# Other ranks for 733 planned steps, and other engines for eleven copies, in a recurrent-attention and token-mixing kernel on one core

## The chip, the core and the metric

The kernel runs on one core of one Trainium2 chip. The metric is the device time of one execution in microseconds (us), lower is better. The core has five instruction queues that run side by side and wait for each other only through semaphores: PE (matmul, with its weight loads shown apart as PEld), DVE (vector), ACT (scalar and activation), POOL (GpSimd) and SP, which here issues the transfers between HBM and on-chip memory. Each queue is strictly in order: an instruction that waits holds everything behind it on its engine.

## What is computed

A decayed linear attention runs over 768 positions for 4 batches of 8 heads of width 48. Its output, with the heads side by side (width 384), goes through a token mixer.

```python
for t in range(S):                       # attention, per batch and head
    cur = einsum('bhd,bhe->bhde', u[None] * kt, vt)
    y[:, :, t] = einsum('bhd,bhde->bhe', rt, state + cur)
    state = wt[:, :, :, None] * state + einsum('bhd,bhe->bhde', kt, vt)
...
wq, wk = x @ w_q, x @ w_k                # mixer, x: [4, 768, 384]
W_tok = (1 / sqrt(64)) * einsum('bsd,btd->bst', wq, wk)
out = maximum(einsum('bst,btd->bsd', W_tok, x), 0) @ w_out
```

## The kernel before

**Tiling.** The work is cut into 12 units of 256 positions (two chunks of 128, called c0 and c1): unit n belongs to batch n // 3. Units 2, 5, 8 and 11 end a batch, and after them the mixer runs for the whole batch. The first and the last unit run chunk by chunk in several steps. In this text "10:KT" is step KT of unit 10, "11:x1" the second chunk of step x, and "5:os2" is step os for the third block of 256 output rows of the batch that unit 5 ends.

**The steps of a unit**, in the order of its data, with the function that issues each:
- Four loads from HBM, w, k, r and v, of 384 KB each. In seven of the twelve units (the string DIRECT) v comes as four transfers of 96 KB (L226), otherwise as one (L230).
- ln (ACT, L467) takes the logarithm of w; cw (PE) sums it along the chunk; en and ep (ACT, L498 and L504) are its exponentials.
- k16 and r16 (L475) cast k and r to bf16. kT and rT (PE) transpose them; ks (a copy, L371 on ACT or L375 on DVE) and qT (DVE, L529) follow.
- RT (DVE, L536) and KT (L547, DVE or POOL) are r and k with their decay. ptm (POOL, L553) is the decay of a chunk.
- v16, vp, vb, or vb alone where v came directly (POOL, L562), make the bf16 tile VB.
- dps (PE), dd (a small copy) and vd (POOL, L601) are the term with u.
- A (PE) and am (DVE, L619) are the masked product inside a chunk; kb (PE) and kd (L373 on ACT, L377 on DVE) the transposed keys; sn (PE) and sb (DVE, L666) the new state; y (PE) and x (DVE, L707) the output of the attention.
- xt (PE), xts (copy), qk (PE), qks (copy; in unit 11 split into qk1 and qk2 for each chunk) begin the mixer.
- At the end of a batch: T (PE) and Ts (ACT, L784), then for each of three blocks mx (PE), rl (L381 ACT, L383 DVE), fp (PE), os (copy) and st, the store of 384 KB (L838).
- "warm" steps are matmuls on zeros that nothing reads.

**What sets the order.** Every step is put on one of the five queues with a rank. The list RANK, written out by hand, gives each step its place: the steps of an engine are issued in the order of their ranks, and ranks are compared only within one engine. The dictionary ENG says, with one letter for each unit (A, D or P for ACT, DVE or POOL), where a step runs that can run on several engines (for rl and os the letter is that of the block). Plan.order() then walks the queues with its own estimates of durations. It can't change the order on an engine, but it hands out the eight PSUM banks by these estimates. The function add (inside unit) registers a step, copy issues it on the engine chosen.

**Buffers.** Loads rotate over four tiles for each input. The output tile os also has four: block m of the whole run (m = 0 to 11) uses tile m mod 4, so 5:os1 (m = 4) can be written only when the store of 2:os0 has left that tile, and 5:os2 when that of 2:os1 has. VB, KT, Vd, dd and their like have two tiles each.

Of the kernel before, what the change touches and what calls it, by code (L numbers as in the profile page):

```python
# [149 lines left out]
def kernel(  # L150
# [137 lines left out]
    for j in range(2):  # L288
# [9 lines left out]
               KT=-956, ptm=-433, v16=-873, vp=-305, vb=-304, dps=-1398, vd=-510, A=-1752,  # L298
               am=2180, kb=370, kd=2179, sn=-276, sb=-57, y=-127, x=-406, xt=-2208, xts=-634,
               qk=796, qks=-45, T=-761, mx=134, rl=-215, fp=-10, os=-8, st=95, stick=-14)  # L300
    ENG = dict(k16="DAPPAPPPPPPP", r16="DPPPPAPPPPPP", KT="DDPDPPPPPPPP", vb="AAAADAAAAAAA",
               kd="AAADAAAAADAA", xts="ADDADAADAAAD", qks="AAADAAAAAAAA", rl="AAAAAAAAAAAA",
               os="AAAAAAADDDDD", dd="AAAAAADDAAAD", ks="DDAAADADDAAD")
    RANK = [14, 0, 0, 0, 0, 15, 0, 0, 0, 1, 0, 0, 2, 0, 0, 5, 0, 0, 0, 0, 1, 1, 3, 1, 5, 2, 5, 10,
            2, 5, 4, 3, 2, 7, 6, 4, 1, 20, 9, 21, 11, 6, 7, 14, 8, 17, 9, 15, 10, 19, 12, 24, 13,
            23, 37, 17, 30, 15, 47, 23, 59, 33, 13, 28, 8, 89, 45, 55, 31, 4, 40, 32, 16, 38, 9,
            6, 11, 46, 75, 2, 3, 29, 69, 91, 43, 25, 7, 68, 3, 0, 0, 4, 0, 0, 6, 0, 0, 9, 0, 0, 4,
            6, 3, 12, 7, 8, 18, 22, 10, 14, 12, 11, 8, 9, 34, 16, 35, 18, 13, 41, 19, 33, 16, 27,
            15, 44, 20, 48, 57, 25, 49, 22, 56, 26, 61, 30, 8, 0, 0, 7, 0, 0, 10, 0, 0, 15, 0, 0,
            13, 5, 10, 36, 19, 17, 26, 39, 14, 21, 18, 14, 12, 16, 50, 24, 17, 54, 24, 51, 23, 52,  # L310
            25, 60, 27, 62, 63, 29, 67, 32, 73, 37, 80, 41, 90, 45, 102, 52, 42, 0, 0, 87, 44,
            104, 53, 49, 0, 0, 109, 56, 114, 59, 53, 0, 0, 12, 0, 0, 11, 0, 0, 17, 0, 0, 18, 0, 0,
            20, 11, 18, 53, 27, 26, 42, 66, 22, 33, 31, 28, 21, 19, 70, 34, 74, 36, 23, 72, 35,
            71, 34, 64, 30, 76, 36, 82, 81, 39, 83, 40, 92, 46, 97, 46, 13, 0, 0, 16, 0, 0, 20, 0,
            0, 22, 0, 0, 21, 29, 22, 58, 28, 31, 65, 79, 32, 38, 37, 20, 26, 25, 84, 42, 27, 88,
            42, 93, 44, 77, 38, 86, 41, 98, 94, 45, 99, 47, 107, 54, 113, 58, 19, 0, 0, 21, 0, 0,
            25, 0, 0, 28, 0, 0, 35, 24, 47, 78, 39, 40, 85, 100, 43, 48, 49, 30, 29, 34, 106, 54,
            35, 110, 56, 117, 58, 101, 51, 115, 57, 121, 122, 61, 128, 66, 133, 69, 139, 74, 149,
            79, 154, 82, 54, 0, 0, 151, 80, 162, 86, 52, 0, 0, 168, 89, 173, 92, 51, 0, 0, 23, 0,
            0, 24, 0, 0, 27, 0, 0, 30, 0, 0, 43, 28, 32, 96, 49, 50, 95, 103, 48, 51, 50, 33, 36,  # L320
            37, 116, 60, 108, 53, 40, 111, 55, 127, 64, 112, 57, 120, 60, 131, 125, 63, 132, 68,
            137, 71, 147, 78, 29, 0, 0, 26, 0, 0, 31, 0, 0, 36, 0, 0, 55, 31, 38, 118, 61, 63,
            105, 119, 52, 59, 65, 41, 43, 46, 124, 67, 47, 134, 69, 140, 72, 130, 68, 138, 70,
            144, 143, 73, 146, 75, 155, 80, 169, 90, 33, 0, 0, 32, 0, 0, 35, 0, 0, 38, 0, 0, 62,
            39, 42, 126, 65, 67, 123, 129, 62, 66, 71, 44, 45, 48, 136, 72, 50, 152, 78, 142, 74,
            135, 73, 148, 76, 156, 157, 81, 171, 91, 175, 93, 184, 101, 191, 104, 197, 107, 55, 0,
            0, 196, 106, 202, 106, 56, 0, 0, 201, 109, 210, 109, 57, 0, 0, 34, 0, 0, 39, 0, 0, 40,
            0, 0, 43, 0, 0, 64, 49, 51, 141, 76, 75, 145, 150, 77, 77, 79, 53, 57, 54, 160, 85,
            158, 83, 61, 163, 84, 159, 82, 161, 83, 166, 85, 177, 172, 90, 178, 92, 183, 100, 190,
            103, 37, 0, 0, 41, 0, 0, 46, 0, 0, 48, 0, 0, 70, 52, 56, 164, 87, 88, 153, 167, 81,  # L330
            86, 88, 59, 60, 62, 179, 95, 65, 174, 91, 181, 93, 176, 94, 182, 94, 188, 187, 97,
            189, 99, 195, 105, 198, 108, 44, 0, 0, 45, 0, 0, 47, 0, 0, 50, 0, 0, 84, 55, 58, 180,
            96, 97, 99, 98, 165, 170, 87, 89, 95, 64, 66, 96, 67, 68, 63, 185, 98, 69, 70, 192,
            100, 194, 101, 186, 102, 193, 102, 199, 200, 103, 203, 105, 206, 111, 108, 104, 204,
            110, 207, 107, 112, 205, 208, 209, 113, 226, 233, 228, 212, 221, 230, 227, 232, 234,
            229, 224, 231, 223, 235, 222, 225, 211, 114, 110, 215, 216, 116, 58, 0, 0, 113, 59, 0,
            0, 214, 115, 111, 217, 218, 118, 60, 0, 0, 114, 61, 0, 0, 213, 117, 112, 219, 220,
            119, 120, 115, 62, 0, 0]
    DIRECT = "001011011011"
    SPLIT = (0, B * NU - 1)  # L340
    NAMES = dict(A="ACT", D="DVE", P="POOL")
# [64 lines left out]
    def unit(n, state, batch):  # L406
# [12 lines left out]
        def add(eng, dur, at, fn, after=(), more=0, fill=None, got=None, cs=(0, 1), use=(), lag=None,  # L419
                mode=0):  # L420

            after = list(after)
            read = []
            for g in use:
                if g is None:
                    continue
                read.append(g.first)
                after += [g.by[c] for c in cs]
            behind = None if got is None else got.first
            if behind is not None:  # L430
                fill = None
            elif fill in ("wg", "rg", "kg", "vg", "lw", "r16", "k16", "ep", "os", "KD"):
                behind = state.get(fill)
            if lag is None:
                lag = 260 if eng == "PE" else 80
            step = plan.add(NAMES.get(eng, eng), dur, STEP * n + OFF[at] + more, fn, after,
                            fill=fill, read=read, lag=lag, mode=mode, behind=behind)
            if fill is not None:
                state[fill] = step
            if got is not None:  # L440
                got.put(step, cs)
            return step
# [29 lines left out]
        def f_c16(dst, src, e):  # L472
            def f():
                op = dict(A=nc.scalar.copy, D=nc.vector.tensor_copy, P=nc.gpsimd.tensor_copy)[e]
                op(view(dst, 0, [[64, H], [512, 2], [1, D]]),  # L475
                   view(src, 0, [[D2, H], [D, 2], [1, D]]))
            return f
        e = ENG["k16"][n]
        add(e, 680 if e == "D" else 830, "c16", f_c16(k16, kg, e), fill="k16", got=g["k16"],
            use=[g["kg"]])  # L480
        e = ENG["r16"][n]
        add(e, 680 if e == "D" else 830, "c16", f_c16(r16, rg, e), more=1, fill="r16", got=g["r16"],
# [38 lines left out]

        kse = ENG["ks"][n]

# [8 lines left out]
        for cs in fine:  # L532
# [9 lines left out]

            kte = ENG["KT"][n]

# [19 lines left out]
        else:  # L564
# [12 lines left out]

            vbe = ENG["vb"][n]

# [12 lines left out]

        dde = ENG["dd"][n]

# [287 lines left out]

    for s, at in zip(plan.steps, RANK):
        s["rank"] = at
# [32 lines left out]
```

## Time and profile before

| | us |
|---|---|
| median of 11 runs | 108.97 |
| lowest, highest run | 107.0, 110.42 |
| the profiled execution | 107.97 |
| its span, first to last instruction | 106.0 |

| engine | busy us of the span | share |
|---|---|---|
| PE (matmul) | 95.1 | 90% |
| DVE | 87.7 | 83% |
| ACT | 80.0 | 75% |
| POOL | 70.4 | 66% |

The profile gives one execution. In its rows a time is the start in us from the first instruction, followed by the duration, engine, line, operation, output and inputs; in square brackets stands how long the engine had been idle before, and what ended that. About 2.0 us of the profiled execution's time lie outside its span. The granted clock of PE was 1.000 throughout.

The 63 entries of SP's queue are the 48 loads, one entry with the weights of the mixer, and 14 stores. From 0.78 to 80.68 us SP issues without a break of more than half a microsecond; all loads and two stores (2:st0 and 2:st1) are in that stretch. The other stores come after.

### The profile page before, as it was taken

To read this page: it belongs to the slowest core of one execution; us is meant where nothing else is said; L and a number is where in the kernel's file an instruction comes from. 1 tells how busy PE (TensorE), PEld (TensorE's weight loads), DVE (VectorE), ACT (ScalarE), POOL (GpSimd) and SP (SyncE) were. 2 spreads that over 40 slices of the span, in tenths; PEclk is the share of its full clock that TensorE was granted. 3 is DMA by queue.
4 is the path that set the end of the run, shared out by engine and by line. 5 is a ranking of instruction groups with operands and counts; after the bars stand their busy time and mean duration, and the time that the engine had idled before them with its cause. 6 is when DMAs were issued, how large, how long until landed. Compare 5 with 4: busy or idle time off the path is not lost.

```text
span 106.0 us, 3708 instructions
## 1 busy us (share of the span) xinstructions
PE 95.1 (90%) x1500; PEld 69.7 (66%) x1506; DVE 87.7 (83%) x138; ACT 80.0 (75%) x123; POOL 70.4 (66%) x92
## 2 busy tenths in 40 slices
PE   5859789997999967999998898799998999998995
PEld 2226665685886755887787666668785887856551
DVE  6898997899999975999899997889998689754740
ACT  4368787897988957997899949888894895954610
POOL 6600859599959929799979985995689599000000
PEclk9999999999999999999999999999999999999999
DMA  2999999999999998989998979999968780033563
GB/s 28 297 325 325 325 323 282 230 276 158 304 295 259 180 271 228 273 151 316 314 315 177 200 142 267 349 290 260 248 158 193 270 336 29 0 152 148 219 244 134
DMA packets 61217, 24.62 MB, mean 232 GB/s; under 512 B 58896, under 2 KB 60048, under 8 KB 61200
## 3 DMA queue, kind: packets, MB, share of 16 engines
q1 hardware_dynamic: 60640, 24.19, 85.5%
q10 hardware_dynamic: 560, 0.20, 0.7%
q8 instruction: 11, 0.18, 0.7%
q14 instruction: 6, 0.05, 0.2%
HBM read 19.66 MB, written 4.72 MB: 230 GB/s over the span
## 4 chain that ended last, share of the span: by engine, by line
PE 40%; DMA 17%; POOL 11%; SPq 10%; DVE 9%; issue 6%; ACT 5%; POOLq 0%; DVEq 0%; ACTq 0%
PE PS L181 40%; DMA vg<-in_v_dram 11%; SPq L226 9%; POOL KT L547 4%; DMA out_dram<-os 4%; POOL Vd L601 3%; DMA wg<-in_w_dram 3%; POOL VB L562 2%; ACT os L371 2%; POOL k L475 1%; DVE RT L536 1%; SPq L230 1%; ACT VB L371 1%; ACT kd L373 1%; DVE SB L666 1%
## 5 line engine op out<-in xcount | busy, mean ns | idle before, releaser
L619 DVE TENSOR_TENSOR AM<-PS,US 128x1024 bf16<-128x1024 f32 x24 | 28.9, 1218 | 1.1 <-PE PS L181 0.6
L547 POOL TENSOR_TENSOR KT<-ks,en 128x1024 bf16<-128x1024 bf16 (+1 forms) x10 | 19.4, 1935 | 1.0 <-PE PS L181 0.6
L601 POOL TENSOR_TENSOR Vd<-VB,dd 128x768 bf16<-128x768 bf16 (+1 forms) x14 | 18.4, 1319 | 2.1 <-ACT dd L371 1.3
L707 DVE SCALAR_TENSOR_TENSOR X<-PS,gx,Vd 128x768 bf16<-128x768 f32 (+1 forms) x13 | 12.3, 955 | 3.7 <-PE PS L181 3.2
L181 PE MATMUL PS<-Z 128*128 128x512 bf16 x45 | 13.8, 422 | 1.5 <-DVE uT L248 1.2
L467 ACT ACTIVATE lw<-wg 128x768 bf16<-128x768 f32 x12 | 10.0, 847 | 6.0 <-DMA wg<-in_w_dram 6.0
L181 PEld LDWEIGHTS <-KT 48*128 48x128 bf16 (+1 forms) x272 | 10.7, 95 | 5.6 <-issue 3.2
L181 PE MATMUL PS<-wo,MX 128*128 128x384 bf16 x72 | 13.5, 326 | 0.1
L666 DVE TENSOR_TENSOR SB<-PS,ptm 128x384 bf16<-128x384 f32 x20 | 11.0, 552 | 2.9 <-PE PS L181 2.6
L504 ACT ACTIVATE ep<-PS 128x1024 bf16<-128x1024 f32 (+1 forms) x14 | 12.7, 922 | 0.6 <-PE PS L181 0.5
L498 ACT ACTIVATE en<-PS 128x1024 bf16<-128x1024 f32 (+1 forms) x14 | 12.5, 903 | 0.7 <-PE PS L181 0.7
L381 ACT ACTIVATE MX<-PS 128x768 bf16<-128x768 f32 (+1 forms) x12 | 8.8, 732 | 2.1 <-PE PS L181 1.9
L181 PE MATMUL PS<-RT,KT 48*128 48x128 bf16 x192 | 9.2, 217 | 1.2 <-POOL KT L547 0.5
L475 POOL CAST r<-rg 128x768 bf16<-128x768 f32 x10 | 8.2, 823 | 2.3 <-DMA rg<-in_r_dram 2.2
L371 ACT COPY os<-PS 128x768 f32<-128x768 f32 (+1 forms) x10 | 7.1, 708 | 3.5 <-PE PS L181 3.3
L181 PEld LDWEIGHTS <-MX 128*128 128x128 bf16 x72 | 6.7, 98 | 3.9 <-issue 0.3
L475 POOL CAST k<-kg 128x768 bf16<-128x768 f32 x9 | 7.4, 824 | 2.6 <-PE PS L181 1.6
L181 PE MATMUL PS<-ID,k 128*128 128x128 bf16 x96 | 7.4, 220 | 1.9 <-DVE k L475 1.2
L373 ACT ACTIVATE kd<-PS,gv 128x384 bf16<-128x384 bf16 (+1 forms) x11 | 8.1, 741 | 1.2 <-PE PS L181 1.2
L181 PEld LDWEIGHTS <-Z 128*128 128x128 bf16 x51 | 5.0, 105 | 6.0 <-issue 2.3
L536 DVE TENSOR_TENSOR RT<-PS,ep 128x1024 bf16<-128x1024 bf16 (+1 forms) x14 | 8.3, 606 | 0.5 <-PE PS L181 0.3
L181 PE MATMUL PS<-VB,AM 128*128 128x48 bf16 x192 | 8.2, 183 | 0.6 <-ACT os L371 0.5
(82 smaller groups left out, 210.0 us busy)
## 6 DMA issues: line engine op xcount, KB each, us to landing
wg<-in_w_dram SPq DMA_DIRECT2D x12, 384.0 KB, 5.3
kg<-in_k_dram SPq DMA_DIRECT2D x12, 384.0 KB, 5.0
rg<-in_r_dram SPq DMA_DIRECT2D x12, 384.0 KB, 5.5
out_dram<-os SPq DMA_DIRECT2D x9, 384.0 KB, 4.2
vg<-in_v_dram SPq DMA_DIRECT2D x28, 96.0 KB, 3.8
vg<-in_v_dram SPq DMA_DIRECT2D x5, 384.0 KB, 5.0
out_dram<-os SPq DMA_DIRECT2D x5, 192.0 KB, 2.7
wof<-in_moe_w_out_dram SPq DMA_DIRECT2D x1, 576.0 KB, 5.9
```

The costliest lines, as they stand in the source:

```text
L181: nc.tensor.matmul(o, l, rr, start=start, stop=stop, skip_group_check=True, is_transpose=trans)
L226: nc.sync.dma_start(out=view(tl, c * DM, [[D, H], [1, D]], p0=64 * j, pn=64), in_=src[j])
L371: nc.scalar.copy(o, i)
L467: nc.scalar.activation(view(lw, 0, [[64, H], [512, 2], [1, D]]), view(wg, 0, [[D2, H], [D, 2], [1, D]]), ACT.Ln, bias=0.0, scale=math.exp( ...
L475: op(view(dst, 0, [[64, H], [512, 2], [1, D]]), view(src, 0, [[D2, H], [D, 2], [1, D]]))
L498: nc.scalar.activation(sb("en", [C, 1024])[:, cols(cs, 512)], t["cw"][:, cols(cs, 512)], ACT.Exp, bias=0.0, scale=-1.0)
L504: nc.scalar.activation(view(ep, cs[0] * NP * EW + 66, [[EW, NP * len(cs)], [-65, 2], [1, 64]]), t["cw"][:, cols(cs, 512)], ACT.Exp, bias=0 ...
L547: e.tensor_tensor(sb("KT", [C, 1024])[:, cols(cs, 512)], t["ks"][:, cols(cs, 512)], t["en"][:, cols(cs, 512)], ALU.mult)
L601: nc.gpsimd.tensor_tensor(sb("Vd", [C, 2 * DM])[:, cols(cs, DM)], t["VB"][:, cols(cs, DM)], view(t["dd"], cs[0] * H, [[1, len(cs) * H], [0 ...
L619: nc.vector.tensor_tensor(view(sb(f"AM{c}", [C, 1024]), 0, [[C, 8], [1, C]]), view(t[f"A{c}"], 0, [[C, 8], [1, C]]), view(US, 0, [[0, 8], ...
L666: nc.vector.tensor_tensor(view(x, 0, [[D, H], [1, D]]), view(t[f"sn{c}"], 0, [[D, H], [1, D]]), view(t["ptm"], c * 8, [[1, 8], [0, D]]), A ...
L707: nc.vector.scalar_tensor_tensor(view(X["t"], (2 * i + c0) * DM, [[DM, ncs], [1, DM]]), view(t["y"], c0 * 512, [[512, ncs], [1, DM]]), gx, ...
```

## The change

It replaces the dictionary ENG and the list RANK. No function, tile or operand is touched.

```diff
-    ENG = dict(k16="DAPPAPPPPPPP", r16="DPPPPAPPPPPP", KT="DDPDPPPPPPPP", vb="AAAADAAAAAAA",
-               kd="AAADAAAAADAA", xts="ADDADAADAAAD", qks="AAADAAAAAAAA", rl="AAAAAAAAAAAA",
-               os="AAAAAAADDDDD", dd="AAAAAADDAAAD", ks="DDAAADADDAAD")
-    RANK = [14, 0, 0, 0, 0, 15, 0, 0, 0, 1, 0, 0, 2, 0, 0, 5, 0, 0, 0, 0, 1, 1, 3, 1, 5, 2, 5, 10,
...
+    ENG = dict(k16="DPPAAPPPPPPP", r16="DPPPPAPPPPPP", KT="DDPDPPPPPPPP", vb="AAAADAAAAAAA",
+               kd="AADDAAAAADAA", xts="DDAADAADAAAD", qks="ADADAAAAAADA", rl="AAAAAAAAAAAA",
+               os="AAAAAAADDDDD", dd="AADAADDAAAAD", ks="DDAAADADDAAD")
+    RANK = [14, 0, 0, 0, 3, 15, 0, 0, 0, 1, 0, 0, 2, 0, 0, 5, 0, 0, 0, 0, 1, 1, 2, 1, 5, 3, 5, 7,
...
```

**Other engines.** Read letter by letter:

| step | from | to |
|---|---|---|
| 1:k16 | ACT | POOL |
| 3:k16 | POOL | ACT |
| 2:kd (its one half) | ACT | DVE |
| 0:xts | ACT | DVE |
| 2:xts | DVE | ACT |
| 1:qks, 10:qks | ACT | DVE |
| 2:dd, 5:dd | ACT | DVE |
| 7:dd | DVE | ACT |

**Other orders.** Sorting the ranks within each engine gives the queues. PE has 236 steps before and after, DVE 116 and 120, ACT 121 and 117, POOL 71 and 71, SP 63 and 63. Most steps move by one to three places. Places in a queue that the prediction speaks of (a semicolon stands where steps that keep their place are left out):

| queue | before | after |
|---|---|---|
| SP, early | 2:k, 2:w, 1:v, 2:r | 1:v, 2:k, 2:w, 2:r |
| SP, middle | 4:r, 5:k, 4:v; 7:k, 6:r | 4:r, 4:v, 5:k; 6:r, 7:k |
| SP, late | 10:k, 2:st0, 9:v, 11:w, 11:k, 10:r, 11:r, 10:v, 2:st1, 11:v | 10:k, 11:k, 9:v, 11:w, 2:st0, 10:r, 11:r, 2:st1, 10:v, 11:v |
| POOL, early | ub, 0:v16, 0:ptm0, 1:r16, 0:ptm1, 2:k16, 0:vd0, 0:vd1, 1:ptm, 1:v16, 2:r16, 3:k16, 2:ptm, 1:vd, 2:KT | 1:k16, 0:ptm0, 0:ptm1, ub, 0:v16, 1:ptm, 1:r16, 1:v16, 0:vd0, 0:vd1, 2:k16, 2:r16, 1:vd, 2:KT, 2:ptm |
| POOL, middle | 5:k16, 4:vb, 4:ptm, 4:vd | 4:ptm, 4:vb, 5:k16, 4:vd |
| POOL, 60 to 70 us | 8:ptm, 7:vb, 7:vd, 8:vb, 9:k16, 8:vd, 9:r16, 10:k16, 9:KT | 7:vb, 7:vd, 8:vb, 8:vd, 9:k16, 9:r16, 8:ptm, 10:k16, 9:KT |
| POOL, late | 10:vb, 11:vb, 11:KT0, 10:vd, 11:ptm0, 11:KT1 | 10:vb, 11:KT0, 10:vd, 11:vb, 11:KT1, 11:ptm0 |
| ACT, late | 5:os2, 8:qks, 10:kd, 10:dd, 11:en0 | 5:os2, 10:kd, 8:qks, 10:dd, 11:en0 |
| DVE, late | 11:am0, 11:am1, 11:sb0, 11:x0, 11:x1, 11:xts, 8:os1, 11:qk1, 11:qk2, 8:os2 | 11:am0, 11:sb0, 11:am1, 11:x0, 11:x1, 11:xts, 10:qks, 11:qk1, 8:os1, 11:qk2, 8:os2 |
| PE, 65 to 68 us | 7:y0, 9:kT, 7:y1, 6:qk | 7:y0, 7:y1, 6:qk, 9:kT |
| PE, late | 8:mx1, 8:fp0, 10:qk, 11:y0, 11:y1, 8:mx2, 8:fp1, 11:xt (two), 11:T (blocks 0 to 3), 11:qk (two), 11:T (4), 11:T (5), 8:fp2, 11:mx0, one warm, 11:mx2, 11:mx1 | 8:mx1, 11:y0, 8:fp0, 11:y1, 8:mx2, 10:qk, 11:xt (two), 8:fp1, 11:qk (two), 11:T (0 to 3), 11:T (4), 11:T (5), 8:fp2, 11:mx0, 11:mx2, 11:mx1 |

On PE the 26 warm steps of the first 42 us stand at other places among the real ones, and just as many remain; of the 16 of the last unit, one moves from between 11:mx0 and 11:mx2 to the end. In PE's queue the steps up to 10:A0 are the same set before and after.

## The prediction

> **What bounds the kernel now.** I read three views: the busy time by stretch, the chain of waits, and the timeline of single engines. First the stretches (busy us of PE, PEld, DVE, ACT, POOL, then clock, DMA share, GB/s):
>
> ```profile
> 43.00:60.00 17.00, 16.13 (x308) 13.47 (x307) 16.19 (x24) 15.87 (x22) 15.93 (x15) 1.00 1.01 246
> 60.00:80.30 20.30, 19.03 (x331) 14.54 (x327) 18.36 (x25) 16.87 (x25) 15.97 (x17) 1.00 0.95 247
> 80.30:93.80 13.50, 13.01 (x233) 10.49 (x233) 10.35 (x15) 10.21 (x18) 8.70 (x11) 1.00 0.54 177
> ```
>
> Until 80 us the DMA share stays near 1.0 and four engines are over 78% busy: no single engine is the bound there. POOL's timeline tells what paces it:
>
> ```profile
> 30.29 0.82 POOL L475 CAST r<-rg 128x768 bf16<-128x768 f32 x1 [0.85 <-DMA rg<-in_r_dram]
> ...
> 66.16 0.83 POOL L475 CAST k<-kg 128x768 bf16<-128x768 f32 x1 [0.93 <-DMA kg<-in_k_dram]
> ...
> 75.86 0.83 POOL L475 CAST r<-rg 128x768 bf16<-128x768 f32 x1 [0.96 <-DMA rg<-in_r_dram]
> ...
> 77.28 0.82 POOL L475 CAST r<-rg 128x768 bf16<-128x768 f32 x1 [0.42 <-DMA rg<-in_r_dram]
> 78.06 2.13 POOL L547 TENSOR_TENSOR KT<-ks,en 128x1024 bf16<-128x1024 bf16 x1
> ```
>
> These are 3:r16, 9:k16, 10:r16, 11:r16 and 10:KT: again and again POOL stands until a load lands. SP issues loads back to back until 80.68, so they are a stream with its own timetable. Compute that arrives earlier waits; compute that arrives later by less than the bracket loses nothing. The last such pin for PE is 11:r16, which holds 10:KT and so 10:A0:
>
> ```profile
> 80.35 0.23 PEld L181 LDWEIGHTS <-KT 48*128 48x128 bf16 x8 [0.32 <-POOL KT L547]
> ...
> 81.45 0.80 ACT L371 COPY os<-PS 128x768 f32<-128x768 f32 x1 [1.41 <-PE PS L181]
> ...
> 82.30 0.56 PE L181 MATMUL PS<-VB,AM 128*128 128x48 bf16 x16 [0.49 <-ACT os L371]
> ...
> 83.17 1.02 DVE L707 SCALAR_TENSOR_TENSOR X<-PS,gx,Vd 128x768 bf16<-128x768 f32 x1 [1.08 <-PE PS L181]
> ```
>
> And the end of the chain of waits:
>
> ```profile
> 77.29 4.08 DMA out_dram<-os
> 81.37 0.02 issue
> 81.40 0.02 ACTq L371
> 81.41 0.04 issue
> 81.45 0.81 ACT os L371
> 82.26 0.04 issue
> 82.30 11.52 PE PS L181 x206
> ```
>
> The reader sees a wait handed down: 2:st1, issued at 77.29 behind all of 10:v, frees its os tile at 81.37. 5:os2 on ACT, whose matmuls ended at 80.36, starts at 81.45. It empties a PSUM bank that 9:y needs, so PE stands 0.49, and 9:x on DVE starts at 83.17. From there PE runs without a wait to 93.8.
>
> **The change, part by part.**
>
> *The loads.* Up to the last one the stream has the same 48 loads, weights and two stores in both versions. It ends at the same time unless SP waits for a tile; each load's tile was last read more than 10 us before its issue, so I cost the stream at nothing. Single moves: 1:v passes two loads (about 1.2 us each by SP's spacing); 2:k and 2:w land that much later, while 2:k16 now stands behind 0:vd, at about 16.9, far after it lands. 4:v in front of 5:k lands some 1.5 us earlier. That takes most of an idle 1.4 us from PE, which stood for VB until 40.37 (4:vb cast at 39.49). 5:k16 falls from 36.72 to about 39.4, with 4:sn0, 4:A0 and two mx (1.3 us of PE) ahead of 5:kT to cover it. But 6:k16 and 7:k16 are tied to landings again, so I carry nothing past 46 us.
>
> *The start, 7 to 27 us.* 1:k16 moves from ACT (0.82) to the head of POOL (0.82) and frees ACT; 1:en can start at about 9.9 for 10.52. DVE has next to no idle time here and gets 0:xts (0.55 on DVE by the row of 1:xts, 0.80 on ACT), half of 2:kd (0.38: an estimate between 0.61 for a whole kd and 0.36 for an XT of the same size) and 2:dd (0.17). DVE also gets 1:qks and 10:qks (0.56 each by 3:qks, 0.50 on ACT) and 5:dd, and gives back 2:xts (0.55) and 7:dd (0.17). Net DVE +1.67, ACT -1.76, POOL 0.
>
> Here a rule speaks against the change. The row first:
>
> ```profile
> 9.23 0.42 DVE L547 TENSOR_TENSOR KT<-ks,en 128x512 bf16<-128x512 bf16 x1
> ...
> 10.69 0.92 DVE L547 TENSOR_TENSOR KT<-ks,en 128x512 bf16<-128x512 bf16 x1
> ```
>
> The same instruction takes 0.50 longer when POOL's cast of 0:v16 runs beside it (10.51 to 11.33). The Trainium skill, SBUF — State Buffer, section "Who interferes with whom", says why: a DVE instruction with two SBUF inputs and a GpSimd instruction that reads SBUF share an interface, and the later one is blocked until the other ends. After the change 1:k16 casts on POOL at 9.4 to 10.2, so 0:KT0 is hit too. The row bounds this: 0 to 0.50 us. By the rule alone it could be the remainder of a 0.82 cast. I take 0.5. With the net 1.1 of copies before 28 us (0.55 + 0.38 + 0.17) the start's price is 1.6 us of DVE, against 0.6 from the earlier en and about 0.9 of DVE idle time there (0.57 before 0:x, 0.30 before 1:x). Net nothing to 0.5 late, covered at 30.29 by the 0.85 that POOL waits for 3:r and at 40.8 by the 1.57 that DVE waits for 4:sn0. Without that cover it costs 0.5.
>
> *The middle, 43 to 80 us.* 9:kT stands behind 7:y1 and 6:qk (0.4 us each by weight loads), which fills the 0.67 that PE idled for 9:k16. 8:ptm goes behind 9:r16, to about 68.4; its reader 8:sb0 ran at 69.08. 7:vd no longer waits there. The 0.3 to 0.7 gained runs into the landings of 10:r and 11:r: nothing.
>
> *2:st1 in front of 10:v.* SP reaches it at 72.65 instead of 77.29; with 4 us to land it is gone by 77, well before 80.4. 5:os2 then starts a microsecond earlier, PE's 0.49 goes, and 9:x starts at about 82.5: -0.65 on DVE. 10:v lands about 1.2 us later (81.6 for 80.4); 10:vb ran at 81.74 behind 9:vd, so that costs 0.1. 2:st0 goes the other way, from 64.66 to the slot of 11:k at 67.74, and lands at about 73.9; 5:os1 started at 75.54. The margin is 1.6.
>
> *The tail.* On DVE from 83.17 to 91.3 there is 0.5 us of idle time, so it follows 9:x: -0.65. Then 11:y0 no longer waits behind 8:fp0 and 10:qk, and 11:x0 follows 11:am1 at once; before, DVE idled 0.57 there. So 11:x1 ends near 91.9 for 93.05. PE has 8:fp1 (1.0) for the gap while 11:xts is copied, and 11:T(0 to 3) for the gap behind 11:qk, where it stood 0.40. 10:qks on DVE costs 0.56 but lies beside 8:fp1. On POOL 11:vb now stands behind 11:KT0 and 10:vd and ends at 87.4 (before 84.1): 11:sn0 read it at 88.33, so this lives on 0.9 of slack. 11:KT1 comes out at 88.6 for 88.39. I give back 0.2. The warm matmul that leaves the mixer's path is worth 0.2 at most; I count 0.
>
> *PSUM banks* are dealt anew. The trace can't show the new deal; the nearest row is the 0.49 above. I take 0 and keep -0.5 to +0.5.
>
> Sum: -0.65 (store), -0.5 (order of y and x), -0.3 (gaps around 11:qk), +0.2 (POOL) = -1.25, from 107.97 to 106.7. The median shown is 1.0 above the profiled execution; in its terms 107.7, and I say 107.8.
>
> One more rule to weigh: Perfetto Trace Analysis, section "Identifying the Most-Contended Engine", says that matmul busy time misleads and weight-load time should be read. By that PE is at 66% and not 90%, DVE with 83% is the most contended, and 1.67 us more on it would make 109.6 where the profiled execution had 107.97. The trace of the last stretch decides otherwise: from 80.3 to 93.8 DVE is busy 10.35 of 13.5, and its first idle 1.08 is a wait for PE.
>
> **The rivals.** *A, the gain is given back in the tail:* 11:KT1 behind 11:vb comes later than reckoned, because 11:KT0 waits for 11:en0 (bracket of 0.41 before), and the last blocks are bound by their own copies. For it: POOL's 4.7 us from 11:en0 to 11:KT1 are serial. Against: DVE needs 11:A1 only after 11:sb0. Time 108.9.
>
> *B, slower: PSUM becomes the wait of the tail.* y, mx and fp take two of the eight banks each, xt and 10:qk one. In the new order 11:y stays open from 11:y0 to 11:x1 across 8:fp0, 8:mx2, 10:qk and 11:xt: 2 + 2 + 2 + 1 + 1, all eight, and 8:fp1 comes next. Banks come free through ACT, in order: rl 0.81, os 0.80, rl 0.81, with 10:xts 0.80 and 11:xts 0.48 between. Each copy that PE waits for in full costs 0.8, with x and T behind it. Two such holds (1.6) eat the 1.25; it decides from the third: +2.4 gives 1.2 above the median, 110.2, a fourth 111. For it: the 0.49 at 82.30 is a hold of this kind, and ACT is the only engine that empties these tiles. Against: before, fp0, 10:qk, y and mx2 held seven and PE ran from 82.30 to 93.8 without one.
>
> *C, the loads don't pin the middle*, and the idle 1.4 at 39 us and 0.67 at 66 are kept: 1.5 us more, 106.3. Against: the brackets of POOL.
>
> **Numbers.** Main case 0.45, A 0.25, B 0.22, C 0.08. A measurement of this kernel tells about 1% from no change, 1.1 us. Faster by over 1%: 0.32 of the main case, C, and 0.02 of A = 0.42. Slower by over 1%: 0.20 of B, 0.03 of A = 0.23. Within 1%: 0.35. The range takes in C and the near end of B: 106.3 to 110.2; the main case alone is 106.9 to 108.6.
>
> **What would show it.** Right: ACT's idle before 5:os2 under 0.3, 10:A0 still at 80.2 to 80.6, 11:x1 ended by 92.3, no PE wait for a copy at the qk of unit 11. Wrong: 10:A0 away from 80.4 by over 0.7 (the loads don't pin it), an ACT wait before 5:os1 (then 2:st0 landed after 75.5), PE waits for rl or os after 88 us, or 11:A1 waiting for POOL.

## The result and the profile after

| | before | after |
|---|---|---|
| median, us | 109.13 (47 runs) | 107.65 (12 runs) |
| lowest, highest | 106.63, 111.7 | 104.73, 109.92 |
| ratio of after to before | | 0.9819, 95% interval 0.9745 to 0.9892 |
| the profiled execution | 107.97 | 107.51 |
| its span | 106.0 | 104.8 |

The runs before are the eleven of the table further up and 36 more. The ratios in this text leave out runs that lay more than 1.5% above the fastest of their kernel (here nine of the twelve after), and since the runs of this kernel spread over 4 us, I also give the means of all runs, with two standard errors. The two dictionaries ENG differ in ten letters, so that ten copies change their engine and not the eleven of the title.

The busy time by stretch, of the kernel after (busy us of PE, PEld, DVE, ACT, POOL, then clock, DMA share, GB/s):

```profile
43.00:60.00 17.00, 15.81 (x304) 13.15 (x299) 15.89 (x23) 16.05 (x23) 16.09 (x17) 1.00 1.00 248
60.00:80.80 20.80, 19.67 (x337) 15.36 (x333) 18.42 (x24) 17.11 (x26) 16.17 (x17) 1.00 1.00 254
80.80:93.80 13.00, 12.95 (x237) 10.46 (x238) 10.94 (x16) 10.44 (x18) 8.74 (x11) 1.00 0.51 173
```

Up to 10:A0 the picture is the old one: the transfers fill the time. In the last row PE is busy for 12.95 of 13.00 us, where it was busy for 13.01 of 13.50. The timeline of single engines of the kernel after, with instructions that the prediction showed of the kernel before, and three that it did not (9:kT at 68.13, 8:ptm at 68.81, 8:sb0 at 69.18):

```profile
67.25 0.82 POOL L475 CAST k<-kg 128x768 bf16<-128x768 f32 x1
68.13 0.45 PEld L181 LDWEIGHTS <-k 128*128 128x128 bf16 x8 [1.14 <-POOL k L475]
68.81 0.22 POOL L553 TENSOR_TENSOR ptm<-ep,MB 128x16 f32<-128x16 bf16 x1
69.18 0.56 DVE L666 TENSOR_TENSOR SB<-PS,ptm 128x384 bf16<-128x384 f32 x1 [0.95 <-POOL ptm L553]
...
76.53 0.83 POOL L475 CAST r<-rg 128x768 bf16<-128x768 f32 x1 [2.71 <-DMA rg<-in_r_dram]
77.88 0.83 POOL L475 CAST r<-rg 128x768 bf16<-128x768 f32 x1 [0.52 <-DMA rg<-in_r_dram]
78.66 2.13 POOL L547 TENSOR_TENSOR KT<-ks,en 128x1024 bf16<-128x1024 bf16 x1
...
80.72 0.80 ACT L371 COPY os<-PS 128x768 f32<-128x768 f32 x1 [0.45 <-PE PS L181]
80.84 0.78 PEld L181 LDWEIGHTS <-KT 48*128 48x128 bf16 x16 [0.55 <-POOL KT L547]
...
83.01 1.02 DVE L707 SCALAR_TENSOR_TENSOR X<-PS,gx,Vd 128x768 bf16<-128x768 f32 x1 [0.50 <-PE PS L181]
```

POOL works ahead and then stands 2.71 us for 10:r: whatever was won between 43 and 73 us ends there. 5:os2 (80.72) now waits for its own matmuls on PE and no longer for the store: 2:st1 had landed at 79.01. And the end of the chain of waits of the kernel after (start, us, what):

```profile
71.31 6.42 DMA rg<-in_r_dram
77.93 0.73 issue
78.66 2.14 POOL KT L547
80.85 15.38 PE PS L181 x255
96.31 0.97 DVE os L375
97.32 3.35 PE PS L181 x19
100.72 3.19 PE PS L181 x14
```

The last transfer in this chain is now 11:r instead of 2:st1. The last two pieces on PE are fp and then the closing warm matmuls, which the last stores do not wait for. I cut each execution into three parts at two marks: the start of 10:A0, and the end of the last copy of unit 11 (11:os1 of the third block, on DVE); the rest is up to the landing of the last store.

| us | before | after | difference |
|---|---|---|---|
| start to 10:A0 | 80.35 | 80.84 | +0.49 |
| 10:A0 to the end of the last copy | 21.71 | 20.20 | -1.51 |
| last copy to the last store landed | 2.92 | 2.07 | -0.85 |
| last store landed to the end of the span | 1.01 | 1.69 | +0.68 |
| outside the span | 1.98 | 2.71 | +0.73 |
| sum | 107.97 | 107.51 | -0.46 |

So the profiled pair shows 2.36 us saved after 10:A0, and 1.90 us lost in three other places. The experiments were to tell which of these five entries belong to the change.

### The profile page after: what moved, and what is told of

Read it like the earlier page. It is cut to its first block, busy times and chain, and to the rows that moved or that the text cites. A ratio compares the mean times of both kernels' runs of the same rounds, so it can differ in the third digit from the quotient of the medians.

```text
span 104.8 us, 3694 instructions
## 1 busy us (share of the span) xinstructions
PE 94.9 (91%) x1498; PEld 70.1 (67%) x1506; DVE 89.2 (85%) x142; ACT 78.7 (75%) x119; POOL 70.6 (67%) x92
## 4 chain that ended last, share of the span: by engine, by line
PE 35%; DMA 30%; DVE 13%; POOL 10%; SPq 4%; ACT 3%; issue 3%; POOLq 0%; DVEq 0%
PE PS L181 35%; DMA rg<-in_r_dram 18%; DMA vg<-in_v_dram 5%; DMA kg<-in_k_dram 3%; POOL KT L547 3%; DVE AM L619 3%; DMA wg<-in_w_dram 3%; POOL r L475 2%; SPq L226 2%; POOL k L475 2%; POOL Vd L601 1%; ACT kd L373 1%; DVE KT L547 1%; DVE qT L529 1%; DVE RT L536 1%
## 5 line engine op out<-in xcount | busy, mean ns | idle before, releaser
L373 ACT ACTIVATE kd<-PS,gv 128x384 bf16<-128x384 bf16 (+1 forms) x10 | 7.5, 748 | 3.1 <-PE PS L181 3.1
L181 PE MATMUL PS<-ID,r 128*128 128x128 bf16 x96 | 7.4, 220 | 1.6 <-POOL r L475 1.6
```

Source lines behind the costliest of these rows:

```text
L181: nc.tensor.matmul(o, l, rr, start=start, stop=stop, skip_group_check=True, is_transpose=trans)
L373: nc.scalar.activation(o, i, ACT.Copy, bias=0.0, scale=by)
```

## The experiments

The runs of one group share the chip and the runs of the kernel before. A kernel has 12 or 13 runs, but e3, e7, e8, e10 and e11 have only six. The granted clock of PE was 1.000 in the 20 us from 10:A0 on in all fourteen profiles, so that no tail below is slower by its clock; ahead of 10:A0 it averaged 0.98 in e2, e5, e8, e11 and e12, and 1.000 in the others. I call the prediction's main case T: the loads pin the kernel until 10:A0, and what counts is what follows.

### One part of the change alone

e1 has the queues of before up to 10:A0 and those of after behind it; e2 the reverse, with SP's loads and first stores of after. e3 is before with one stretch of SP's queue from after. e4 is after with twelve os tiles, so that no os copy ever waits for a store, and with 2:st0 and 2:st1 behind the last load. Apart from what is shown, only RANK differs, and in e2 10:qks is on ACT as before. In the cuts of code an ellipsis stands for the rest of a line.

```diff
# e1, against before
-  ... qks="AAADAAAAAAAA", ...
+  ... qks="AAADAAAAAADA", ...
# e3, against before: SP's queue
-  10:k, 2:st0, 9:v, 11:w, 11:k, 10:r, 11:r, 10:v, 2:st1, 11:v
+  10:k, 11:k, 9:v, 11:w, 2:st0, 10:r, 11:r, 2:st1, 10:v, 11:v
# e4, against after
-    NOS = 4
+    NOS = 12
-  11:k, 9:v, 11:w, 2:st0, 10:r, 11:r, 2:st1, 10:v, 11:v
+  11:k, 9:v, 11:w, 10:r, 11:r, 10:v, 11:v, 2:st0, 2:st1
```

e1:

> All queues as before up to 10:A0 (the loads and the two early stores of SP too), from there on as in the changed kernel, 10:qks on DVE with it. Theory T, the loads pin the kernel until 10:A0 and only the order behind it counts: 10:A0 within 0.5 us of where the kernel before has it, the stretch from there to the end 1.0 to 1.5 us shorter than its 25.6, ratio to before 0.986 to 0.993; ACT's wait before 5:os2 of about 1 us stays. Rival M, the new orders of the start and the middle bring it: ratio 0.998 to 1.003.

e2:

> The other half: all queues as in the changed kernel up to 10:A0, SP's loads and two early stores included, and as before from there. Theory T: 10:A0 where it was, a stretch to the end at most 0.6 us shorter (the store's wait is gone), ratio 0.993 to 1.001. Rival M: ratio 0.982 to 0.988.

e3:

> The kernel before with one thing changed, SP's late order: 11:k and 2:st0 change places around 9:v and 11:w, and 2:st1 goes in front of 10:v. By the sum in the prediction: no ACT wait over 0.3 us before 5:os2, no PE wait before 9:y, 9:x 0.65 us earlier, ratio 0.993 to 0.997. If the wait before 5:os2 was slack: the wait goes and the time stays, ratio 0.999 to 1.002.

e4:

> The changed kernel with twelve os tiles for four, and 2:st0 and 2:st1 behind the last load. It tests the pin itself: two stores of 1.2 us each leave the load stream in front of 11:v. If the loads pin 10:KT: 11:r lands 1.0 to 1.5 us earlier (one store stood before it), 10:A0 at 79.2 to 79.9, the time 0.8 to 1.5 us under the changed kernel's, ratio to before 0.968 to 0.975. If the engines themselves are the bound before 80 us: 11:r lands earlier, 10:A0 stays at 80.4 to 80.9, ratio 0.980 to 0.984.

The kernel before had a median of 107.6 in 29 runs here. The last three columns are of the one profile of each kernel.

| | median | mean against before | ratio, 95% interval | 10:A0 | to last copy | to landing |
|---|---|---|---|---|---|---|
| e1 | 107.53 | +0.23 ± 0.88 | 1.0012, 0.9961 to 1.0062 | 81.02 | 21.30 | 4.03 |
| e2 | 108.18 | +0.77 ± 0.96 | 1.0056, 0.9993 to 1.0120 | 80.57 | 21.14 | 2.72 |
| e3 | 108.46 | +0.69 ± 0.79 | 1.0109, 1.0034 to 1.0185 | 81.50 | 21.06 | 2.77 |
| e4 | 106.73 | -0.97 ± 0.52 | 0.9979, 0.9931 to 1.0027 | 80.12 | 20.20 | 2.06 |

Three things follow. First, e2 and e3, with the tail of before and the stores earlier, need 21.1 us from 10:A0 instead of 21.71: that is the store's wait, 0.57 to 0.65. Still neither is faster, and the ratio of e3 lies above both ranges given for it. Why is not shown; 10:A0 and the rest vary by more than this wait. Second, e4 has the tail of after to the hundredth, 20.20, but its times miss both forecasts: 11:r landed at 75.91, 1.8 us earlier than in the kernel after, and 10:A0 came only at 80.12, with a ratio of 0.9979. Third, e1 has every engine's order of after in the tail and still needs 1.10 us more than after, so that most of the gain is lost. By its ratio alone e1 looks like rival M (the gain comes from the orders before 10:A0), but e2, which has these orders, is far from the 0.982 to 0.988 of M. The timeline of PE tells why e1 loses. In the kernel after, 8:fp0 follows 11:y0 directly:

```profile
90.10 1.14 PE L181 MATMUL PS<-wo,MX 128*128 128x384 bf16 x6
```

In e1 it has a bracket:

```profile
91.06 1.14 PE L181 MATMUL PS<-wo,MX 128*128 128x384 bf16 x6 [0.53 <-ACT MX L382]
```

Order is not all that a rank sets: Plan.order() deals out the PSUM banks by its own estimates. Working that deal out for both kernels, 8:fp0 gets banks 6 and 7 in after, while 8:mx1 has 4 and 5. In e1 both get 5 and 6, so that 8:fp0 waits until ACT's 8:rl1 (90.19, 0.81 us) has emptied them. From the end of 11:am1 to the end of 11:x1 e1 takes 2.06 us, after takes 1.38: 0.68 of the 1.10. Another 0.33 lies behind 11:Ts, where PE waits 0.23 for an os copy (at 98.26). The first is the hold that rival B was built on, once, at a price of 0.7.

### The same chip again, and what the loads cover

e5 is the changed kernel unaltered, beside before on another chip. e6 is before with twelve os tiles and the two stores behind the loads. e7 and e8 are before with the multiplication by the mask issued twice in one unit, two more DVE instructions of 1.2 us: in unit 3, long before the last loads, or in unit 10, behind them.

```diff
# e6, against before
-    NOS = 4
+    NOS = 12
-  2:st0, 9:v, 11:w, 11:k, 10:r, 11:r, 10:v, 2:st1, 11:v
+  9:v, 11:w, 11:k, 10:r, 11:r, 10:v, 11:v, 2:st0, 2:st1
# e7 (unit 3) and e8 (unit 10), against before
             def f_am(c=c):
-                nc.vector.tensor_tensor(
+                for _ in range(2 if n == 3 else 1):
+                    nc.vector.tensor_tensor(
...
```

e5:

> The changed kernel, unaltered, beside the kernel before on one chip, because the kernel before has shown medians from 107.6 to 109.1 us. Theory T (the last 25 us are shorter by 1.0 to 1.5 us, whatever the loads do): ratio 0.985 to 0.991, and from 10:A0 to the end of the last copy 20.0 to 20.5 us where the kernel before has 21.7. Rival N (the gain measured was the spread of the load stream): ratio 0.996 to 1.004.

e6:

> The kernel before with twelve os tiles for four, and 2:st0 and 2:st1 behind the last load; all other orders as before. If the two stores in the load stream cost it their time, and the wait for the tile costs the rest: 11:r lands about 1.2 us earlier (at 75.9 to 76.5), no wait before 5:os2, 10:A0 at 79.2 to 80.0, ratio 0.985 to 0.992. If PE is the bound there and not the loads: 10:A0 at 80.0 to 80.4 and ratio 0.993 to 0.998, by the wait that is gone alone.

e7:

> The kernel before with 3:am issued twice for each chunk, 2.4 us more on DVE at 34 us. Theory T (what happens before 80 us is absorbed where engines wait for loads): 10:A0 at most 0.4 us later than in the kernel before, ratio 0.998 to 1.004. Rival M (the middle is bound by the engines and passes on what it loses): 10:A0 1.0 to 2.4 us later, ratio 1.009 to 1.022.

e8:

> The same double work in the last stretch: 10:am issued twice for each chunk, 2.4 us more on DVE at 81 to 87 us. Theory T: the first 1.2 us fall into DVE's idle 1.08 before 9:x, the second push 10:x, 11:am and 11:x one for one: 11:x1 ends 1.0 to 1.6 us later counted from 10:A0, ratio 1.008 to 1.014. If PE alone bounds this stretch: under 0.4 us later, ratio under 1.004.

The kernel before had a median of 108.0 in 23 runs.

| | median | mean against before | ratio, 95% interval | 10:A0 | to last copy | to landing |
|---|---|---|---|---|---|---|
| e5 | 107.61 | +0.16 ± 0.81 | 1.0063, 1.0011 to 1.0114 | 79.38 | 20.20 | 4.01 |
| e6 | 106.87 | -0.38 ± 0.81 | 0.9980, 0.9928 to 1.0031 | 80.43 | 21.06 | 4.10 |
| e7 | 107.57 | +0.37 ± 1.29 | 1.0110, 1.0050 to 1.0171 | 80.55 | 21.05 | 2.92 |
| e8 | 109.65 | +2.06 ± 0.75 | 1.0305, 1.0235 to 1.0374 | 81.43 | 22.72 | 2.71 |

e7 and e8 are the test of the cover. In the timelines of e7 (DVE, then PEld) the added work is there, four products in a row instead of two, and 10:A0 comes at 80.55, 0.20 later than in the profile before:

```profile
34.86 4.86 DVE L620 TENSOR_TENSOR AM<-PS,US 128x1024 bf16<-128x1024 f32 x4
...
80.55 0.23 PEld L181 LDWEIGHTS <-KT 48*128 48x128 bf16 x8 [0.32 <-issue]
```

In e8's timeline of DVE one such pair stands in the tail, and the tail is 22.72 instead of 21.05:

```profile
81.95 2.48 DVE L620 TENSOR_TENSOR AM<-PS,US 128x1024 bf16<-128x1024 f32 x2 [0.29 <-PE PS L181]
```

In the traces, the 2.4 us of DVE at 35 us move 10:A0 by less than it varies from run to run. The closest comparison is e6, which has no added work: 11:r lands there at 76.28 (76.35 in e7) and 10:A0 starts at 80.43. The same 2.4 us behind 10:A0 lengthen the tail by 1.7. By the times, e8 is 2.06 us slower, more than the 1.4% expected at most, and e7 is undecided: its ratio, 1.0110, lies in the range of rival M (1.009 to 1.022) and outside that of T (0.998 to 1.004), while its median is 0.4 us less. So the cover is supported by the traces and not shown by the times. e6 itself, with a ratio of 0.9980 and 10:A0 no earlier than before, fits the expectation that PE's own work holds 10:A0 there.

e7 also shows that the store's wait is not always there: with SP's queue of before, 2:st1 landed at 79.44 and 5:os2 waited for PE only (0.36). The same holds for e1 and e8, and for e9 further down: of the five profiles with this queue, only the one that the prediction read has the wait. The tail without that wait is 21.06, 21.06, 21.05 in e3, e6 and e7.

And e5 does not repeat the gain: its ratio, 1.0063, is nearer to the 0.996 to 1.004 of rival N (the gain was the spread of the loads) than to the 0.985 to 0.991 of T. The changed kernel has the same median in both comparisons, 107.65 and 107.61. The kernel before had 109.13 in the first and 107.38 to 108.0 in the three groups here, so that the gain on record owes as much to the longer times of before in that comparison; what made them longer is not shown. In the profile, e5's tail is the one promised (20.20) and 10:A0 is early, but the last stores land late. The page of e5, DMA queues, then issues with the median time to landing:

```profile
q8 instruction: 12, 0.20, 0.8%
...
out_dram<-os SPq DMA_DIRECT2D x5, 192.0 KB, 4.0
```

Before has 2.7 in the place of 4.0, the kernel after 1.9, and both pages count 11 packets on q8. In the kernel after, as in e2, e4, e7 and e8, a twelfth starts only behind the span's end (at 106.55). In e1, e5 and e6, and in none of the other profiles, a packet of 16,384 bytes on q8 falls among the last stores (at 102.40, 99.03 and 101.65 us), and one of the 16 shares of a store lands late: of the store that e5 issued at 98.15, fifteen shares landed from 99.84 to 100.04 and one at 102.19. The packets of q8 come once in some 250 matmuls and weight loads of PE (248 in before, 256 in e5, on average), and by this count the twelfth belongs to the closing warm matmuls. A late share can come without such a packet too: of the store that e2 issued at 94.56, one share landed 1.1 us behind the other fifteen.

### Without the closing warm matmuls

That led to the last group. A second look at the ends says that the closing warm matmuls matter even where no packet disturbs. Timeline of PE, before:

```profile
101.30 3.40 PE L181 MATMUL PS<-Z 128*128 128x512 bf16 x15
```

and after:

```profile
100.29 3.62 PE L181 MATMUL PS<-Z 128*128 128x512 bf16 x15
```

Before, they end at 104.70 and the last store lands 0.28 later, at 104.98. After, they end at 103.91 and the last store had landed at 103.11. In all ten profiles with them, the span ends 1.0 to 1.1 us behind the store or 0.9 behind the warm matmuls, whichever is later.

e9 and e10 are before and after without the sixteen warm matmuls of unit 11. e11 is e4 without them. e12 is e11 with 10:A0 and 10:kb ahead of 5:fp2 on PE, and 10:en ahead of 5:os1 on ACT.

```diff
# e9 and e10, against before and after
-            mm(stile(F32, "warm"), Z[:, ds(0, C)], Z)
+            if count != 16:
+                mm(stile(F32, "warm"), Z[:, ds(0, C)], Z)
# e12, against e11: PE's queue
-  5:fp2, 10:A0, 10:kb
+  10:A0, 10:kb, 5:fp2
# e12, against e11: ACT's queue
-  5:os1, 10:en
+  10:en, 5:os1
```

e9:

> The kernel before without the 15 warm matmuls at PE's end and the one between 11:mx0 and 11:mx2 (they read zeros and nothing reads them; no part of the output is left out). Theory W: the twelfth packet of PE's instruction queue (16 KB, about one per 256 PE instructions) falls among the closing warm matmuls, lies on one of the 16 DMA engines while the last stores move, and so makes the last store land 2 us later in part of the executions. Then no such packet stands between the last store's issue and its landing here, the last store lands 2.0 to 3.0 us after the last copy, and the median lies 0.5 to 1.0 us under the kernel before, with a narrower spread. Rival: the late share is not tied to PE's instructions: median within 0.3 us of before, the spread unchanged.

e10:

> The changed kernel without its 16 closing warm matmuls. Theory W: last store 2.0 to 3.0 us after the last copy, median 0.5 to 1.0 us under the changed kernel with them (107.6 on the last chip), narrower spread. And against the kernel before without them, which shares the chip: T (the new tail is worth a fixed 0.85 us, the wait for the store another 0.66 in part of the executions): 0.8 to 1.5 us less, from 10:A0 to the last copy 20.2 us against 21.1 to 21.7. Rival N (the change brings nothing once the closing stores are undisturbed): within 0.3 us of it.

e11:

> The changed kernel with twelve os tiles, 2:st0 and 2:st1 behind the last load, and without the closing warm matmuls. If the two stores in the load stream delay the last loads by about 1.2 us: 11:r lands by 76.3, 10:A0 at 80.1 to 80.3 (then held by PE's own work and no longer by the loads), median 0.3 to 0.9 us under the same kernel with four tiles. Rival: the loads' landing varies by chance, and the place of the stores is worth nothing: 10:A0 anywhere from 79.4 to 81.5, median equal.

e12:

> The kernel with twelve os tiles and no closing warm matmuls, with 10:A0 and 10:kb ahead of 5:fp2 on PE, and 10:en ahead of 5:os1 on ACT. If PE's order holds 10:A0 once the loads don't: 10:A0 at 79.2 to 79.8, but 5:fp2 is then still to do, so that the end gains only what PE stood idle before: 0 to 0.4 us less than with the old order. If the loads still hold it: 10:A0 unchanged, and the median equal or up to 0.3 us worse (5:os2 later).

The kernel before had a median of 107.38 and a mean of 107.63 in 23 runs.

| | median | mean against before | ratio, 95% interval | 10:A0 | to last copy | to landing |
|---|---|---|---|---|---|---|
| e9 | 107.0 | -0.71 ± 0.78 | 0.9939, 0.9883 to 0.9994 | 81.34 | 21.07 | 2.85 |
| e10 | 105.31 | -2.47 ± 0.93 | 0.9735, 0.9656 to 0.9814 | 78.96 | 20.20 | 2.05 |
| e11 | 105.57 | -2.15 ± 1.40 | 0.9715, 0.9622 to 0.9808 | 81.44 | 20.21 | 2.06 |
| e12 | 107.52 | -0.11 ± 0.67 | 0.9976, 0.9926 to 1.0026 | 79.87 | 22.11 | 2.05 |

e10 is the fastest kernel of the study together with e11, and the clean comparison: against e9 its mean is 1.76 ± 0.99 us lower. In the profiles the tail is 0.87 shorter and the last stores land 0.80 sooner (2.85 to 2.05), which is as much; 10:A0 lies another 2.4 apart. For this pair rival N (within 0.3 us) falls, with six runs of e10. Against after itself there is no run on one chip; through the kernel before, e10's ratio of 0.9735 stands beside 0.9819 and beside the 1.0063 of e5. The page of e10 has one packet less on q8 than e5's, and its stores land in 1.9 us:

```profile
q8 instruction: 11, 0.18, 0.6%
...
out_dram<-os SPq DMA_DIRECT2D x5, 192.0 KB, 1.9
```

The end of its chain is now the last copy:

```profile
78.96 15.39 PE PS L181 x255
94.43 0.97 DVE os L375
95.44 3.15 PE PS L181 x18
98.61 0.56 DVE os L375
```

Theory W is only half borne out. No packet of q8 stands among the last stores in these four profiles, and none lands late. But e9 gains 0.4 in its median where 0.5 was the least expected, and the spread does not narrow (a standard deviation of 1.06 us beside 1.17). Three late landings in ten profiles with warm matmuls and none in four without also happen by chance about one time in four (0.7 to the fourth power is 0.24), so that the packet's part is likely, not shown.

e11 misses its 10:A0 by more than a microsecond, and its median is equal to e10's: the place of 2:st0 and 2:st1 is worth nothing that these times can tell.

e12 misses the other way. 10:A0 came early (79.87) as expected, and the kernel is slower. (5:fp2 lies behind the mark here, so its 22.11 is not comparable with 20.21.) PE's timeline of e12 at 10:A1:

```profile
84.08 0.40 PE L181 MATMUL PS<-RT,KT 48*128 48x128 bf16 x8 [0.45 <-DVE X L709]
```

and of e11:

```profile
84.04 0.39 PE L181 MATMUL PS<-RT,KT 48*128 48x128 bf16 x8
```

The instruction before it, 11:cw, starts 0.58 earlier in e12 (83.01 against 83.59), and at 10:A1 nothing of that is left. Worked out from the kernel, its banks are 2 and 3 in e12, the ones of 9:y, which 9:x on DVE has to empty (83.01 to 84.03); in e11 they are 6 and 7, and 9:y has 0 and 1. Again the deal of the banks took what was gained, here with another order too. Why e12's mean is 2.05 ± 1.39 above e11's, when its one profile ends only 0.3 later, stays open.

## Why the prediction was right, and where it was not

107.8 was forecast and 107.65 measured, inside the range, and the likeliest side (faster by over 1%) came. That it came so close is in part luck. The same two kernels show no gain in e5, and the profiled execution fell by 0.46 where the sum has 1.25: 2.36 saved behind 10:A0, 1.90 lost in terms that the sum did not have. Of the four signs of being right only the last came: 5:os2 waited 0.45 (under 0.3 was asked), 10:A0 started at 80.84 (80.2 to 80.6), 11:x1 ended at 92.34 (92.3), and PE had no wait at the qk of unit 11. None of the signs of being wrong came in this profile; in that of e5 one did, with 10:A0 at 79.38, over 0.7 away from 80.4.

**The store, -0.65: right in mechanism and size for this profile.** 2:st0 landed at 74.72 (73.9 forecast) and 5:os1 started at 75.53 without waiting for it. 2:st1, issued at 72.63 as forecast, took 6.4 us to land and not 4, and was still in time. From 10:A0 to 9:x there were 2.82 us before and 2.17 after, 0.65 less. What the prediction did not know is that the wait is an accident of some executions: e1, e7, e8 and e9 keep the old queue at this point and do not have it. Over many runs the term is worth less than 0.65.

**The order of y and x, the gaps at 11:qk, POOL: -0.5, -0.3, +0.2 forecast, sum -0.6; -0.87 measured** (21.07 in e9 without the store's wait to 20.20). Timeline of DVE, before:

```profile
91.91 1.14 DVE L707 SCALAR_TENSOR_TENSOR X<-PS,gx,Vd 128x384 bf16<-128x384 f32 x2 [0.57 <-PE PS L181]
94.12 0.36 DVE L375 COPY XT<-PS 128x384 bf16<-128x384 bf16 x1 [1.07 <-PE PS L181]
...
97.12 0.96 DVE L375 COPY os<-PS 128x768 f32<-128x768 f32 x1 [1.45 <-PE PS L181]
```

and after:

```profile
89.28 0.55 DVE L666 TENSOR_TENSOR SB<-PS,ptm 128x384 bf16<-128x384 f32 x1
89.75 1.21 DVE L619 TENSOR_TENSOR AM<-PS,US 128x1024 bf16<-128x1024 f32 x1
90.88 0.61 DVE L707 SCALAR_TENSOR_TENSOR X<-PS,gx,Vd 128x384 bf16<-128x384 f32 x1
91.72 0.62 DVE L707 SCALAR_TENSOR_TENSOR X<-PS,gx,Vd 128x384 bf16<-128x384 f32 x1 [0.24 <-PE PS L181]
92.72 0.36 DVE L375 COPY XT<-PS 128x384 bf16<-128x384 bf16 x1 [0.38 <-PE PS L181]
93.12 0.56 DVE L375 CAST qk<-PS 128x384 bf16<-128x384 f32 x1
93.95 0.22 DVE L375 CAST qk<-PS 128x64 bf16<-128x64 f32 x1 [0.27 <-PE PS L181]
```

I count from 10:A0, e9 against after. 11:am0 ends at 8.75 and 8.53: -0.22, since 11:A0 now stands ahead of 8:mx0 on PE, which the sum did not have. From there to the end of 11:x1 it is 3.31 and 2.97: -0.34 for the -0.5 of y and x. 11:x0 waits no longer, but 11:sb0 (89.28) now stands in front of 11:am1. From there to the end of 11:Ts it is 3.56 and 3.41: -0.15, half of the -0.3 forecast, although 1.07 of waiting before 11:xts became 0.38. 10:qks lay beside 8:fp1 (92.61 on PE) as forecast: 11:qk1 behind it (93.95) waited for PE. The rest, -0.15, is behind 11:Ts and in no term. It is not the warm matmul: with it (before) this piece is 5.44, without it (e9) 5.45, so counting 0 was right. POOL's +0.2 did not come: 11:KT1 is out 7.99 behind 10:A0 for 7.43, and no engine waited for it. So the sum of the three is nearer than its parts.

**"I cost the stream at nothing", 10:A0 "still at 80.2 to 80.6": the step that failed.** The traces of e6 and e7 support the cover. But its edge is not a fixed time: over fourteen profiles 11:r lands between 75.39 and 78.12 us and 10:A0 starts between 78.96 and 81.50, with after itself at 80.84 and at 79.38 (e5). That is more than the whole sum. The means of the two kernels swing by as much against each other, -1.59 ± 0.89 in the comparison on record and +0.16 ± 0.81 in e5; that the one makes the other is likely, not shown. Nor do the loads alone hold 10:A0: in e4, with 11:r at 75.91, 10:KT was out at 79.38 and 10:A0 started only at 80.12, behind PE's own work, and in e2, e6, e7 and e11 it was likewise out 0.7 us before.

**The end of the kernel: a missing step.** The sum stopped at the tail's last copy. The last six stores came in a bunch before, five issued from 100.76 to 102.16, and evenly after, about 0.5 apart: -0.85, not foreseen. Against that, the prediction looked at the one warm matmul in the mixer's path and counted 0, and did not look at the fifteen behind it. Before, these ended 0.28 ahead of the last store. After, they end behind it and set the end: +0.68 in the span. The +0.73 outside the span is not a cost of the change: the other eleven runs of the changed kernel have 1.73 to 2.10 us there, and of the 75 runs of the kernel before in the three groups 16 have over 2.2. In the 36 runs of e9 to e12, without closing warm matmuls, it never passes 2.01.

**Two small steps were wrong and covered.** PE's idle 0.67 at 9:kT was to be filled, and became 0.86 (for its weight loads, 0.81 became 1.14): PE reached it earlier, while 9:k16 moved from 66.16 to 67.25. 8:ptm came at 68.81, as forecast near 68.4, but DVE was ready for 8:sb0 by then and waited 0.95. Both lie ahead of the 2.71 that POOL stands for 10:r.

**The start.** 0:KT0 was hit as forecast, but by 0.26 and not 0.5, and 0:KT1 by 0.39 and not 0.50, so that the collision cost 0.15 more than before. Timeline of DVE, after:

```profile
9.84 0.68 DVE L547 TENSOR_TENSOR KT<-ks,en 128x512 bf16<-128x512 bf16 x1
...
11.11 0.81 DVE L547 TENSOR_TENSOR KT<-ks,en 128x512 bf16<-128x512 bf16 x1
```

By the Trainium skill, SBUF — State Buffer, section "Who interferes with whom", the wait lasts while POOL's instruction does. The traces agree nearly: POOL's casts (9.42 and 10.82, 0.82 each) had 0.40 and 0.53 to run when these two started, and in the row of before 0.64; in each case the instruction grew by 0.14 us less than this remainder. So it is the remainder of the cast that counts, and the prediction took over the row of before instead. 1:en started at 9.70, forecast 9.9.

**The rivals.** A (11:A1 late through POOL) did not happen. B did not happen in the changed kernel: PE has no wait for a copy from 80.8 to 93.8. But e1 and e12 show that its mechanism is real and costs 0.6 to 0.7 a time; a chance for it was right. That the deal was good is luck as far as the prediction goes: no view of before shows it, though it can be worked out from the two kernels, as above for e1. C (1.5 us more kept from the middle) did not happen: in both profiles of the changed kernel 10:A0 came 3.1 to 3.3 us behind the landing of 11:r, as before.

## What to carry to other kernels

Behind a stretch that transfers pace, count only what lies after the last wait for a load, and expect the edge itself to move from run to run: here by 1.9 us between profiles with equal queues, more than the 1.25 us of the sum, so that one profile's tail (20.20 or 20.21 us in all five that have its order and no hold) told more than twelve times. Follow every engine to its own last instruction, those with no reader too: work that is harmless 0.28 us before the end becomes the end when the rest gets shorter. And where buffers are dealt by a planner's estimates, a new order is also a new deal, which can be worked out before anything runs; in e1 the same order with another deal gave the gain away.

## What the hardware showed that was not expected

A queue of the DMA engines that the kernel never uses, called an instruction queue on the page and by its count PE's, has 11 or 12 packets of 16,384 bytes in an execution, each 0.9 to 1.9 us long. Where one fell among the last stores, each time a sixteenth of a store landed late (2.2 us in e1 and e5, 1.6 in e6); whether both were on the same DMA engine the trace does not say. With SP's queue unchanged, 11:r landed up to 1.9 us apart between profiles: at 75.84 in e10, 76.08 in e5 and 77.73 in after.
